# Attention and mixture of experts on one core: row stores released inside the score products, weight splits and half row sums on GpSimd

## The chip, the cores and the metric

The kernel runs on one core of a Trainium2 chip. The metric is the device time of one execution in microseconds (us). Before the change it is 597.46 us, the median of 3 runs (596.34 to 598.12). Engines are named as in the profile: PE is TensorE's matmuls, PEld its weight loads, DVE is VectorE, ACT ScalarE, POOL GpSimd, SP the engine that issues most loads.

## The reference

Two stages. Attention works on chunks of 64 tokens, 8 batches of 8 heads with 576 tokens of 64 values. Its output, 4608 rows of 512, goes to 8 experts, one for each row:

```python
scores = scale * np.matmul(q_c, k_c.transpose(0, 1, 2, 4, 3))
scores = scores - np.max(scores, axis=-1, keepdims=True)
attn = np.exp(scores)
attn = attn / (np.sum(attn, axis=-1, keepdims=True) + 1e-09)
out = np.matmul(attn, v_c)
...
expert_idx = np.argmax(logits, axis=1)
...
for e in range(E):
    mask = expert_idx == e
    xe = x[mask]
    h = np.maximum(xe @ w1[e], 0.0)
    ye = h @ w2[e]
    out[mask] = gate_w[mask, None] * ye
```

## The kernel before

**Stages.** The attention loop has 18 iterations, numbered `g` from 0 to 17. Each takes two tiles of 128 rows. A short tail follows in which the last tiles are routed while TensorE already multiplies for the first expert slot, and then the expert stage: slots of 256 rows, grouped by expert through an index table, with the weights loaded per slot. Rows are written to `xd` in DRAM by an indirect DMA that GpSimd issues (`store`, L435), so that they lie in the order of their experts, and are gathered again for the slots (L558).

**Order.** PE, DVE, ACT and POOL run the program in the order in which it is written. Only SP's queue of loads is put in order by the scheduler. Each engine works its queue strictly from the front, so an instruction that waits holds up all behind it.

**One iteration.** The loop is a pipeline. Iteration `g` computes the score products of its own tiles (`scores`, L240, into the tile `psS`, which lies in two PSUM banks), transposes the softmax of iteration `g-1` (L285, copied to `at` by ACT, L286), transposes the rows of iteration `g-2` (L317, copied to `xT`, L319), multiplies attention and v for `g-1` (L294), and computes the gate's logits for `g-2` (L329, copied to `lp`, L968). The product with `sel_g` (L959) at the start of an iteration, behind the score products on PE, reads the `lp` of the iteration before.

The softmax is spread over three engines. DVE takes the row maxima `mx` from `psS` (L253) and subtracts them into `ex` (L256); ACT computes Exp in place (L262). In the next iteration DVE sums the rows of `ex` (`soft_c`, L266) into `su`, ACT adds 1e-9 to the 16 sums (`soft_e`, L272), DVE takes the reciprocal `ri` (L277) and scales the products into a row buffer (L306). DVE then does a few small steps of the routing (L357 to L412, L493 to L525), up to five between the subtraction and `ri` and some more behind L306.

On ACT the order in an iteration is: two copies `at`, two copies `xT`, `soft_e`, Exp, the casts of weights (L86), `lp`, small routing steps, and then the first instruction of the next iteration's store.

**Stores.** From iteration 7 on, two row tiles that are routed are stored in each iteration. So that they don't leave early, ACT first copies one value of the new score tile into an unused last column of the first of the two rows (L433), which the DMA reads. It is called right behind `scores(g)`.

**First weights.** The weights of the first slot arrive in 16 pieces of 128x512 in two buffers `raw` (L981, one load in each of iterations 0 to 6, the others from iteration 12 on in the program's text). `split_half` turns each into a high part (ACT, L86) and a low part, which POOL subtracts at once (L88, same iteration). The tables `loads` and `splits` give the iterations: one piece in each of 1 to 8, one in 14, two in 15 and two in 16.

In iteration 15, right behind that iteration's stores, POOL also issues the first gather, `gather(0)` (L558, two DMAs), which reads rows of `xd` that the stores just ahead of it write, and whose target is a buffer that those stores read.

Of the kernel before, what the change touches and what calls it, by code (L numbers as in the profile page):

```python
# [8 lines left out]
F32 = mybir.dt.float32  # L9
# [4 lines left out]
ALU = mybir.AluOpType  # L14
AX = mybir.AxisListType
# [3 lines left out]
P = 128  # L19
# [6 lines left out]
NG = NTILE // G  # L26
# [12 lines left out]
XW = D + 16  # L39
# [8 lines left out]
def attn_moe_kernel(ctx: ExitStack, tc: tile.TileContext, q, k, v, wg, w, out):  # L48
    nc = tc.nc

    const = ctx.enter_context(tc.tile_pool(name="const", bufs=1))
# [16 lines left out]
    raw = [wpool.tile([P, 2048], F32, name=f"raw{c}") for c in range(2)]  # L68
# [11 lines left out]
    def split_half(j, eng):  # L80

        c, m = j // 2, j % 2
        hi, lo = w_hi[0][c][:, m * 512:(m + 1) * 512], w_lo[0][c][:, m * 512:(m + 1) * 512]
        o = (c % 2) * 1024 + m * 512
        src = raw[j // 4 % 2][:, o:o + 512]
        nc.scalar.copy(hi, src)  # L86
        yield
        eng.tensor_tensor(lo, src, hi.bitcast(F32), ALU.subtract)  # L88
# [133 lines left out]
    def quads(i, hp):  # L222
        for c in range(2):
            for m in range(2):
                o = hp * 128 + c * 64
                yield (slice(c * 64, (c + 1) * 64), m, slice((i * 4 + hp) * 64, (i * 4 + hp + 1) * 64),
                       slice(m * 64, (m + 1) * 64), slice(o, o + 64), (m * 64, c * 64))
# [7 lines left out]
    def scores(g):  # L235
        ps = pair
        for i in range(G):
            for hp in range(4):
                for po, m, fo, pi, fi, at_ in quads(i, hp):
                    nc.tensor.matmul(ps[po, m, fo], qt[g][pi, i, fi], kb[g % NK][pi, i, fi],  # L240
                                     start=True, stop=True, tile_position=at_)
        return ps

    NH = 2 * G * 4

    def heads(x):

        return x.rearrange("p m (h k) -> p (m h) k", k=64)

    def soft_a(ps):  # L250
        mx = sm.tile([P, NH, 1], F32, name="mx", bufs=2)
        ps3 = heads(ps)
        nc.vector.tensor_reduce(mx.rearrange("p h o -> p (h o)"), ps3, AX.X, ALU.max)  # L253

        ex = sp.tile([P, NH // 2, 2, 64], F32, name="ex", bufs=2)
        nc.vector.tensor_tensor(  # L256
            ex.rearrange("p h m k -> p m h k"), ps.rearrange("p m (h k) -> p m h k", k=64),
            mx.rearrange("p (m h) o -> p m h o", m=2).broadcast_to([P, 2, NH // 2, 64]), ALU.subtract)
        return ex
# [1 line left out]
    def soft_b(ex):  # L261
        nc.scalar.activation(ex, ex, AF.Exp, scale=0.125)  # L262

    def soft_c(ex):
        su = sm.tile([P, NH, 1], F32, name="su", bufs=2)
        nc.vector.tensor_reduce(su.rearrange("p (m h) o -> p m (h o)", m=2),  # L266
                                ex.rearrange("p h m k -> p m h k"), AX.X, ALU.add)
        return su

    def soft_e(su):  # L270
        suf = su.rearrange("p h o -> p (h o)")
        nc.scalar.activation(suf, suf, AF.Copy, bias=1e-9)  # L272
# [7 lines left out]
    def attn_t(ex, banks="UV"):  # L280
        at = sp.tile([P, G, 4, 128], F32, name="at", bufs=1)
        for i in range(G):
            pt = bank(banks, [P, 4, 128])
            for hp in range(4):
                nc.tensor.transpose(pt[:, hp, :], ex[:, i * 4 + hp, :, :].rearrange("p m k -> p (m k)"), ident)  # L285
            nc.scalar.copy(at[:, i, :, :], pt)  # L286
        return at
# [24 lines left out]
    def x_t(g, xt):  # L312
        xT = sp.tile([P, 4, G * P], F32, name="xT1", bufs=1)
        for i in range(G):
            pxt = bank("TQ", [P, 4, 128])
            for kc in range(4):
                nc.tensor.transpose(pxt[:, kc, :], xt[:, (g * G + i) % RB, kc * 128:(kc + 1) * 128],  # L317
                                    ident)
            nc.scalar.copy(xT[:, :, i * P:(i + 1) * P], pxt)  # L319
        return xT  # L320
# [103 lines left out]
            active.append([g, next(g), True])  # L424

    waiting = []

    def store(n, after=None):

        for k, (b, i, t, di) in enumerate(waiting[:n]):  # L430
            x = xb[t // RB % XB][:, t % RB, :]
            if k == 0 and after is not None:
                nc.scalar.copy(x[:, XW - 1:XW], after)  # L433
            stored.add(t)
            nc.gpsimd.indirect_dma_start(  # L435
                out=xds[t],
                out_offset=bass.IndirectOffsetOnAxis(ap=di[:, i, :], axis=0),
                in_=x, in_offset=None, bounds_check=NT - 1, oob_is_err=False)
        del waiting[:n]
# [4 lines left out]
    def advance(kind, side=False):  # L444


        for x in active:
            if x[1] == kind and x[2] == side and not (kind == "t" and r_live[0]):
                x[1] = next(x[0], "end")
                if x[1] == "end":  # L450
                    active.remove(x)
                return
# [493 lines left out]

    cpl = const.tile([P, E + 2 * NU], F32, name="cpl")

    st_e, st_l, st_x = {}, {}, {}
    pls = [None]  # L950

    def sel_(g):
# [18 lines left out]
    def pauses():  # L971
        for x in list(active):
            if x[1] is None:
                x[1] = next(x[0], "end")
                if x[1] == "end":
                    active.remove(x)
# [9 lines left out]
    def cast(g):  # L986

        for j in splits.get(g, ()):
            list(split_half(j, nc.gpsimd))
        for j in loads.get(g, ()):  # L990
            load_q(j)

# [2 lines left out]
    for g in range(NG):  # L995
        ga, gl = g - 1, g - 2
        pace[0] = 1000
        ps = scores(g)
        keep((12, 6, 0)[min(g, 2)])

        store(2 if g + 1 < NG else 4, ps[:, 0, 0:1])
        if gl >= 1:
            sel_(gl - 1)
            advance("c")
        if ga >= 0:
            at = attn_t(st_e[ga])
            su = soft_c(st_e.pop(ga))
        if gl >= 0:
            st_x[gl] = x_t(gl, xb[gl * G // RB % XB])
        if ga >= 0:  # L1010
            soft_e(su)
        st_e[g] = soft_a(ps)
        if g + 1 < NG:
            soft_b(st_e[g])
        else:

            c2.close()
            psum.append(ctx.enter_context(tc.tile_pool(name="psum", bufs=1, space=PSUM)))
        pauses()
        cast(g)  # L1020
        advance("t")
        if g + 1 < NG:
            small_op(5)
        if ga >= 0:
            px = attn_v(ga, at)
        logits(gl)
        if g + 1 == NG:
            soft_b(st_e[g])
        if ga >= 0:
            ri = soft_d(su)  # L1030
            x_out(ga, px, ri, xb[ga * G // RB % XB])
        small_op(2)
        advance("a")
        side_op(4)
        if g + 3 < NG:
            load_qk(g + 3)
        if 3 <= g + 2 < NG:
            load_v(g + 2)

    g = NG - 1  # L1040
# [4 lines left out]
    ex = st_e.pop(g)  # L1045
    at = attn_t(ex, "TQ")
    filler(1)
    su = soft_c(ex)
    soft_e(su)
    advance("a")  # L1050
# [240 lines left out]
```

## Time and profile before

One execution was profiled. Its own time is 601.14 us, its span, from the first to the last instruction, 599.2 us, at a mean granted TensorE clock of 0.976.

| What | Value |
|---|---|
| median of 3 runs | 597.46 us |
| profiled execution: time, span | 601.14 us, 599.2 us |
| HBM read, written | 121.60 MB, 19.82 MB |
| split by POOL (L88), 128x512 | 13 times, 1277 ns each |
| row stores (L435) | 36 DMAs, 0.97 to 1.15 us of POOL each |
| score products start (iteration 0, iteration 17) | 4.78 us, 124.97 us |

How to read the rows in the prediction: a group's row has line, engine, operation, output and inputs with shapes, count, then busy time in all and mean time of one in ns, then the idle time of the engine just before them and what ended it. A row of the timeline has its start, its length, engine, line, operation, and in brackets the idle time before it and what released it. "issue" means that the engine waited for nothing that the profile shows. Matmul records in a row of scores count 64 for the 32 products of an iteration, two for each.

### The profile page before, as it was taken

What the parts mean: (1) busy time and instruction counts of PE and PEld (TensorE: products, weight loads), DVE (VectorE), ACT (ScalarE), POOL (GpSimd) and SP (SyncE); (2) the same over time, 40 slices, a digit from 0 to 9 for tenths busy, and PEclk for the clock granted to TensorE, in tenths of its full rate; (3) what the DMA queues carried; (4) which work ended last, traced back from release to release, by engine and by line L of the source; (5) the groups of instructions that cost most, each with busy time, mean ns of one, the idle gap of its engine ahead of it and who ended that gap; (6) DMA issues with size and microseconds to landing.
All of it is one profiled execution on the core that took longest, in us unless ns stands there. A gap on an engine that the chain in (4) does not pass through costs nothing.

```text
span 599.2 us, 14785 instructions
## 1 busy us (share of the span) xinstructions
PE 563.4 (94%) x5603; PEld 497.4 (83%) x5603; DVE 445.9 (74%) x849; ACT 299.3 (50%) x562; POOL 261.2 (44%) x276
## 2 busy tenths in 40 slices
PE   7788788988999999999999999999998999999995
PEld 4676667776889889989899888998997899899894
DVE  7769687896668687786677678788655878777975
ACT  2656464675124555554455455555434555555552
POOL 3214332385645355434364445535424263464352
PEclk9989797999899999999999999999999999999998
DMA  8989897833467462357226622358633135623021
GB/s 296 383 306 333 285 373 231 294 117 142 160 205 250 144 225 81 108 175 230 59 68 235 205 58 71 103 190 319 217 93 99 45 112 191 205 76 101 20 57 37
DMA packets 59701, 103.31 MB, mean 172 GB/s; under 512 B 16240, under 2 KB 32624, under 8 KB 55984
## 3 DMA queue, kind: packets, MB, share of 16 engines
q0 software_dynamic: 20704, 60.74, 30.0%
q1 hardware_dynamic: 38864, 40.94, 21.2%
q8 instruction: 67, 1.10, 0.8%
q14 instruction: 66, 0.54, 0.3%
HBM read 121.60 MB, written 19.82 MB: 236 GB/s over the span
## 4 chain that ended last, share of the span: by engine, by line
PE 61%; DMA 10%; issue 2%; POOL 2%; POOLq 1%; DVE 1%; ACT 1%; ACTq 0%
PE psS L624 15%; DMA out_y<-y,oid 10%; PE psS L631 7%; PE psV L703 5%; PE psU L703 4%; PE psU L704 4%; PE psL L624 4%; PE psU L705 4%; PE psV L704 4%; PE psV L705 4%; PE psL L631 2%; POOLq L1229 1%; PE psK L717 1%; PE psK L719 1%; POOL out_y L731 1%
## 5 line engine op out<-in xcount | busy, mean ns | idle before, releaser
L78 DVE TENSOR_TENSOR wlo<-raw,whi 128x1024 fp32r<-128x1024 f32 x134 | 163.7, 1221 | 27.0 <-ACT whi L77 18.2
L77 ACT CAST whi<-raw 128x1024 fp32r<-128x1024 f32 x134 | 140.1, 1046 | 0.2 <-issue 0.2
L540 POOL DMA_INDIRECT raw<-in_w,widx x70 | 78.6, 1123 | 101.1 <-DVE wlo L78 37.2
L645 ACT ACTIVATE hh<-psS 128x256 fp32r<-128x256 f32 x110 | 42.3, 384 | 160.9 <-PE psS L624 105.3
L731 POOL DMA_INDIRECT out_y<-y,oid x40 | 50.5, 1262 | 112.3 <-ACT y L728 31.2
L624 PE MATMUL psS<-xhi,whi 128*128 128x256 f32 x344 | 98.0, 285 | 0.2 <-issue 0.2
L624 PE MATMUL psS<-xlo,whi 128*128 128x256 f32 x344 | 97.8, 284 | 0.3 <-DVE xlo L583 0.3
L624 PE MATMUL psS<-xhi,wlo 128*128 128x256 f32 x344 | 97.6, 284 | 0.0
L558 POOL DMA_INDIRECT xg<-xd,idx x58 | 71.4, 1231 | 28.9 <-issue 18.5
L650 DVE SCALAR_TENSOR_TENSOR hl<-psS,hh 128x256 fp32r<-128x256 f32 x110 | 46.4, 422 | 42.8 <-ACT hh L645 25.2
L624 PEld LDWEIGHTS psS<-xhi,whi 128*128 128x128 f32 x344 | 66.0, 192 | 4.0 <-issue 0.4
L624 PEld LDWEIGHTS psS<-xlo,whi 128*128 128x128 f32 x344 | 66.1, 192 | 3.3 <-DVE xlo L583 0.5
L624 PEld LDWEIGHTS psS<-xhi,wlo 128*128 128x128 f32 x344 | 66.0, 192 | 0.0
L703 PE MATMUL psU<-whi,hh 128*128 128x512 f32 x144 | 57.4, 398 | 1.6 <-ACT whi L77 1.6
L703 PE MATMUL psV<-whi,hh 128*128 128x512 f32 x144 | 57.9, 402 | 0.8 <-issue 0.6
L704 PE MATMUL psU<-wlo,hh 128*128 128x512 f32 x144 | 57.1, 397 | 0.0
L704 PE MATMUL psV<-wlo,hh 128*128 128x512 f32 x144 | 56.7, 394 | 0.0
L705 PE MATMUL psV<-whi,hl 128*128 128x512 f32 x144 | 56.4, 392 | 0.0
L705 PE MATMUL psU<-whi,hl 128*128 128x512 f32 x144 | 56.4, 392 | 0.0
L435 POOL DMA_INDIRECT xd<-xb,di x32 | 31.6, 986 | 39.3 <-issue 26.2
L88 POOL TENSOR_TENSOR wlo<-raw,whi 128x512 fp32r<-128x512 f32 x13 | 16.5, 1277 | 47.4 <-ACT whi L86 33.9
L240 PEld LDWEIGHTS psS<-kb,qt 64*64 64x64 f32 x1152 | 19.5, 135 | 18.1 <-issue 12.6
(252 smaller groups left out, 1209.5 us busy)
## 6 DMA issues: line engine op xcount, KB each, us to landing
kb<-in_k SPq DMA_DIRECT2D x36, 256.0 KB
qt<-in_q SPq DMA_DIRECT2D x36, 256.0 KB
vb<-in_v SPq DMA_DIRECT2D x36, 256.0 KB
xg<-xg SPq DMA_DIRECT2D x256, 32.0 KB
raw<-in_w SPq DMA_DIRECT2D x16, 256.0 KB
raw<-in_w,widx POOLq DMA_INDIRECT x70
xg<-xd,idx POOLq DMA_INDIRECT x58
out_y<-y,oid POOLq DMA_INDIRECT x40
```

What stands on the lines that cost most here:

```text
L77: nc.scalar.copy(hi, src)
L78: nc.vector.tensor_tensor(lo, src, hi.bitcast(F32), ALU.subtract)
L540: nc.gpsimd.indirect_dma_start(out=raw[c][:, :], out_offset=None, in_=w, in_offset=bass.IndirectOffsetOnAxis(ap=widx[:, u, c:c + 1], axis= ...
L558: nc.gpsimd.indirect_dma_start(out=t[:, :], out_offset=None, in_=xd[0:rows, :], in_offset=bass.IndirectOffsetOnAxis(ap=place(u, h), axis=0 ...
L624: nc.tensor.matmul(ph, a, b[:, kc, 0:BLK], start=kc + i == 0, stop=kc + i == 5)
L631: nc.tensor.matmul(ph, a[par][kc][:, f * 128:(f + 1) * 128], b[:, kc, 0:BLK + n], start=kc + i == 0, stop=kc + i == 5)
L645: nc.scalar.activation(hh, ph, AF.Relu)
L650: nc.vector.scalar_tensor_tensor(hl, ph, 0.0, hh.bitcast(F32), ALU.max, ALU.subtract)
L703: nc.tensor.matmul(py, hh, wh, start=f == 0, stop=False)
L704: nc.tensor.matmul(py, hh, wl, start=False, stop=False)
L705: nc.tensor.matmul(py, hl, wh, start=False, stop=f == 7)
L731: nc.gpsimd.indirect_dma_start(out=outs[m], out_offset=bass.IndirectOffsetOnAxis(ap=oid[u % 3][0:n, m:m + 1], axis=0), in_=y, in_offset=No ...
```

## The change

Five edits, all in the attention loop:

1. `store` is called inside `scores`, behind the first four of the 32 products, instead of behind all of them. In `store` POOL copies the marked column into a small tile `relay` before it issues the DMAs.
2. POOL adds the two halves of each row of `ex` (32 values each) into a quarter of a `raw` buffer that is free at that time (`halve`), behind the Exp of the same iteration.
3. DVE's `soft_c` sums these 32 values instead of 64.
4. `soft_c` and `soft_e` stand behind `soft_a` (maximum and subtraction) of the new scores instead of ahead.
5. POOL's subtraction for a weight piece is issued one iteration after ACT's cast. The copies of ACT stay where they were.

```diff
@@ scores
+                if i == 0 and hp == 0:
+                    store(2 if g + 1 < NG else 4, ps[:, 0, 0:1])
         return ps
...
+    def halve(g, ex):
+
+        c, j = (1, 3) if g < 6 or 12 < g < 15 else (0, 3 if g < 15 else 0)
+        h = raw[c][:, j * 512:(j + 1) * 512].rearrange("p (h m k) -> p h m k", m=2, k=32)
+        nc.gpsimd.tensor_tensor(h, ex[:, :, :, 0:32], ex[:, :, :, 32:64], ALU.add)
+        return h
+
-    def soft_c(ex):
+    def soft_c(h):
         su = sm.tile([P, NH, 1], F32, name="su", bufs=2)
         nc.vector.tensor_reduce(su.rearrange("p (m h) o -> p m (h o)", m=2),
-                                ex.rearrange("p h m k -> p m h k"), AX.X, ALU.add)
+                                h.rearrange("p h m k -> p m h k"), AX.X, ALU.add)
...
+    relay = const.tile([P, 1], F32, name="relay")
...
                 nc.scalar.copy(x[:, XW - 1:XW], after)
+                nc.gpsimd.tensor_copy(relay, x[:, XW - 1:XW])
...
         for j in splits.get(g, ()):
-            list(split_half(j, nc.gpsimd))
+            casts.append(split_half(j, nc.gpsimd))
+            next(casts[-1])
...
-        store(2 if g + 1 < NG else 4, ps[:, 0, 0:1])
...
         if ga >= 0:
-            at = attn_t(st_e[ga])
-            su = soft_c(st_e.pop(ga))
+            at = attn_t(st_e.pop(ga))
         if gl >= 0:
             st_x[gl] = x_t(gl, xb[gl * G // RB % XB])
+        st_e[g] = soft_a(ps)
         if ga >= 0:
+            su = soft_c(st_h.pop(ga))
             soft_e(su)
-        st_e[g] = soft_a(ps)
...
         pauses()
+        for x in casts:
+            next(x, None)
+        casts.clear()
         cast(g)
+        if g + 1 < NG:
+            st_h[g] = halve(g, st_e[g])
```

PE has the same rows in the same order; what differs is a wait. Here is PE's queue at the score products of iteration 7, the first with a store, with the semaphores that a row waits for. Before:

```order
L240 MATMUL psS<-kb_128,qt 64x64 [waits DMAHW7_49,DMAHW0_49,DVE_49]
L240 MATMUL psS<-kb_128,qt 64x64 x15
L240 MATMUL psS<-kb_128,qt 64x64 [waits DMAHW2_49,DMAHW1_49]
L240 MATMUL psS<-kb_128,qt 64x64 x15
L959 MATMUL psL<-sel_g,lp 128x8 [waits Activation_49]
L959 MATMUL psL<-sel_g,lp 128x8
L285 MATMUL psU<-ident,ex 128x128 [waits DVE_49]
```

And after, where L971 is the former L959 and L294 the former L285:

```order
L240 MATMUL psS<-kb_128,qt 64x64 [waits DMAHW7_49,DMAHW0_49,DVE_49]
L240 MATMUL psS<-kb_128,qt 64x64 x3
L240 MATMUL psS<-kb_128,qt 64x64 [waits Activation_49]
L240 MATMUL psS<-kb_128,qt 64x64 x11
L240 MATMUL psS<-kb_128,qt 64x64 [waits DMAHW2_49,DMAHW1_49]
L240 MATMUL psS<-kb_128,qt 64x64 x15
L971 MATMUL psL<-sel_g,lp 128x8 x2
L294 MATMUL psU<-ident,ex 128x128 [waits DVE_49]
```

The fifth product now waits for ACT, which reads the score tile for the store's copy, and the wait ahead of `sel_g` is gone. ACT's own rows and their order are the same in both.

DVE at the change from iteration 15 to 16, before (`add` and `g` are routing steps):

```order
L306 TENSOR_TENSOR xb_125<-psV,ri 128x2x256
L516 TENSOR_SCALAR add_239<-c_1833 128x1
L522 TENSOR_SCALAR add_239<-add_239 128x1
L525 TENSOR_SCALAR g_241<-pid_h,add_239 128x3
L266 TENSOR_REDUCE su<-ex 128x16
L253 TENSOR_REDUCE mx<-psS 128x16
L256 TENSOR_TENSOR ex<-psS,mx 128x2x8x64
L357 TENSOR_REDUCE lm<-lg 128x4
```

And after, with L255, L258 and L275 for the former L253, L256 and L266:

```order
L315 TENSOR_TENSOR xb_125<-psV,ri 128x2x256
L527 TENSOR_SCALAR add_240<-c_1853 128x1
L533 TENSOR_SCALAR add_240<-add_240 128x1
L536 TENSOR_SCALAR g_242<-pid_h,add_240 128x3
L255 TENSOR_REDUCE mx<-psS 128x16
L258 TENSOR_TENSOR ex<-psS,mx 128x2x8x64
L275 TENSOR_REDUCE su<-raw_66 128x16
L366 TENSOR_REDUCE lm<-lg 128x4
```

The sum has moved behind the subtraction and reads what POOL wrote into `raw`.

POOL from the stores of iteration 15 on, through the first gather, to the routing of iteration 16 (`ft` is a routing value that POOL copies into the rows). Before:

```order
L435 DMA xd<-xg_64,di 4608x528 x2
L558 DMA xg_64<-xd,idx_235 128x528 x2
L88 TENSOR_TENSOR wlo_4_80<-raw_66,whi_4_72 128x512
L88 TENSOR_TENSOR wlo_5_81<-raw_66,whi_5_73 128x512
L414 COPY xg_64<-ft 128x2x2
```

And after, with L444 to L446 for the store, L270 for `halve` and L569 for the gather:

```order
L444 COPY relay<-xg_64 128x1
L446 DMA xd<-xg_64,di 4608x528 x2
L569 DMA xg_64<-xd,idx_236 128x528 x2
L88 TENSOR_TENSOR wlo_4_80<-raw_66,whi_4_72 128x512
L270 TENSOR_TENSOR raw_66<-ex 128x512
L423 COPY xg_64<-ft 128x2x2
```

One split instead of two stands behind the gather, and behind it the addition for iteration 15, whose result DVE reads in iteration 16.

More of the change, by code (lines that the diff above doesn't have):

```diff
@@ L947, in attn_moe_kernel @@
     cpl = const.tile([P, E + 2 * NU], F32, name="cpl")
-    st_e, st_l, st_x = {}, {}, {}
+    st_e, st_h, st_l, st_x = {}, {}, {}, {}
+    casts = []
     pls = [None]
```

## Prediction

> **What bounds the kernel now.** I read the page first, then busy time stage by stage, then the chain that ended last inside the one stage that the change edits, then the rows at its stalls. From the page, the share of each engine and the 40 slices:
>
> ```profile
> PE 563.4 (94%) x5603; PEld 497.4 (83%) x5603; DVE 445.9 (74%) x849; ACT 299.3 (50%) x562; POOL 261.2 (44%) x276
> ...
> PE   7788788988999999999999999999998999999995
> ...
> PEclk9989797999899999999999999999999999999998
> DMA  8989897833467462357226622358633135623021
> ```
>
> A slice is 15 us. From slice 11 on TensorE is busy to 9 tenths or more; the expert stage, which the change doesn't touch, follows at its pace. What the attention loop (the first nine slices, 18 iterations, to about 132 us) ends later or earlier is therefore carried to the end one for one. The question is what sets the pace there. Busy time by stretch, one iteration of the loop each (length first, then PE, PEld, DVE, ACT, POOL busy with counts, granted clock, DMA share, GB/s):
>
> ```profile
> 63.28:70.97 7.69, 7.69 (x158) 6.81 (x157) 5.17 (x11) 4.78 (x11) 3.05 (x4) 0.64 0.86 278
> 70.97:77.17 6.20, 5.80 (x170) 5.06 (x165) 5.90 (x13) 3.86 (x10) 2.79 (x6) 1.00 0.73 239
> 77.17:83.73 6.56, 5.64 (x164) 4.75 (x157) 5.66 (x8) 3.75 (x8) 1.96 (x2) 1.00 1.01 380
> ...
> 93.18:101.47 8.29, 8.29 (x167) 7.57 (x166) 5.22 (x15) 4.09 (x10) 2.41 (x5) 0.62 0.59 200
> 101.47:107.59 6.12, 5.71 (x161) 4.71 (x156) 5.19 (x9) 3.75 (x8) 1.96 (x2) 1.00 0.91 304
> ...
> 113.64:120.71 7.07, 6.17 (x172) 5.21 (x166) 6.74 (x15) 4.73 (x13) 2.79 (x3) 1.00 0.76 273
> ```
>
> In iterations 9 and 13 (the rows from 70.97 and from 101.47) TensorE has 0.4 us of idle time in 6.2 and 6.12: its own program sets the spacing, with VectorE close behind. In the last iterations VectorE and then ScalarE take over, as the chain that ended last shows:
>
> ```profile
> 121.25 1.12 DVE su L266
> 122.37 1.14 DVE mx L253
> 123.53 1.24 DVE ex L256
> 124.79 1.06 ACT ex L262
> ...
> 126.26 0.61 ACT whi L86
> 126.88 0.28 ACT lp L968
> 127.20 0.61 PE psL L959 x4
> ```
>
> Row sum, maximum, subtraction, Exp, two weight casts, the copy lp, and only then TensorE's next product. The first 93 us have a third limit: TensorE stops in the middle of a run of products, where no semaphore is awaited (the releaser is "issue"), in stretches where DMA is full (1.01 and 380 GB/s in the row from 77.17).
>
> ```profile
> 62.88 0.47 PE L240 MATMUL psS<-kb,qt 64*64 64x64 f32 x2 [3.81 <-issue]
> ...
> 87.98 0.27 PE L294 MATMUL psU<-vb,at 64*64 64x64 f32 x1 [1.56 <-issue]
> ...
> 92.89 0.36 PE L240 MATMUL psS<-kb,qt 64*64 64x64 f32 x1 [2.21 <-issue]
> ```
>
> At 62.88 only the last 2 of 64 score records were missing, so it isn't a late q or k. After the two long ones the clock falls (0.64 in the row from 63.28, 0.62 in that from 93.18).
>
> **The change, part by part.** All times below are positions in the profiled execution; its span is 599.2 and its time 601.14, 3.7 above the median of 597.46, so I carry only the difference over to the median.
>
> *VectorE's row sum of half the width.*
>
> ```profile
> L266 DVE TENSOR_REDUCE su<-ex 128x16 f32<-128x1024 f32 x17 | 20.6, 1210 | 1.1 <-ACT ex L262 1.1
> L306 DVE TENSOR_TENSOR xb<-psU,ri 128x512 f32<-128x512 f32 x15 | 10.4, 692 | 8.7 <-PE psV L294 5.6 <-PE psU L294 2.5
> ```
>
> A sum over 512 elements isn't in the trace. Half of 1210 ns is 0.60; no gain at all is 1.21; VectorE's pass over 512 elements at L306 takes 0.69. I take 0.67, so 0.54 us less in each of 17 iterations: 9.2 us of VectorE's time. It reaches the end only where VectorE is the last to arrive, and the next part takes that away.
>
> *The store's copy inside the score products.* The order shows that from iteration 7 on the fifth product waits for ScalarE: the 1-column copy reads the score tile that the products still write. Before, only the maximum waited for the copy, and it was usually later anyway.
>
> ```profile
> 76.08 1.16 PE L240 MATMUL psS<-kb,qt 64*64 64x64 f32 x64
> ...
> 77.31 0.16 ACT L433 COPY xb<-psS 128x1 f32<-128x1 f32 x1 [0.56 <-PE psS L240]
> ...
> L240 PE MATMUL psS<-kb,qt x1152: 218/218/366, 4.8 to 125.9; 64*64 64x64 f32 x192
> ```
>
> TensorE must let the first products drain (0.22, one record), the copy begins 0.07 after the last product ends (76.08 + 1.16 = 77.24 to 77.31) and takes 0.16, and TensorE resumes about 0.05 later, as it does after lp in the chain (127.16 to 127.20). That is **0.50 us per iteration** in which TensorE stands still with everything queued behind: the other products, the transposes, attention times v. The bounds are 0 (nothing held) and the time until ScalarE's queue gets there, next part.
>
> *Row sum moved behind the subtraction, Exp behind it.* ScalarE's order is unchanged: the small su step (L272) still stands ahead of Exp. So Exp now waits for the halved sum (0.67), a hand-over (0.08) and the spacing from su to Exp (0.12): 0.87 later after the maximum than before. Behind Exp stand casts, lp and the copy that TensorE now awaits:
>
> ```profile
> 118.30 1.06 ACT L262 ACTIVATE ex<-ex 128x1024 f32<-128x1024 f32 x1 [1.32 <-DVE ex L256]
> 119.26 1.12 ACT L86 CAST whi<-raw 128x512 fp32r<-128x512 f32 x2
> 120.29 0.36 ACT L968 COPY lp<-psL 128x256 f32<-128x256 f32 x1
> ...
> 120.68 0.17 ACT L433 COPY xg<-psS 128x1 f32<-128x1 f32 x1
> ```
>
> This closes a loop from the end of one set of products to the end of the next: 0.05 to the maximum, 2.51 to Exp as before (122.28 to 124.79), 0.87 more, 2.38 from Exp to the store's copy with two casts (118.30 to 120.68), 0.21 for copy and hand-over, and the other 56 of 64 records, 1.02. That is 7.04 us with two casts (iterations 15 and 16), 6.52 with one (a cast is 0.52, half of 119.26 to 120.29), 6.01 with none.
>
> *GpSimd.* An addition of 128x512 is not there, but the split's subtraction of the same size is: 1277 ns. I take 1.27; the bounds are 0.6 and 2.5 (a strided read at half the rate). In most iterations POOL has room for it (1.96 to 3.05 us busy of 6 to 8, in the rows above) and the split, now an iteration late, is needed much later. The exception is iteration 15, where the addition queues behind a gather that waits for row stores to land:
>
> ```profile
> 116.05 0.98 POOL L435 DMA_INDIRECT xd<-xg,di  x1 [0.30 <-issue]
> 120.95 1.05 POOL L558 DMA_INDIRECT xg<-xd,idx  x1 [3.92 <-DVE add L516]
> 122.31 1.01 POOL L558 DMA_INDIRECT xg<-xd,idx  x1 [0.30 <-PE psV L285]
> 123.35 2.51 POOL L88 TENSOR_TENSOR wlo<-raw,whi 128x512 fp32r<-128x512 f32 x2
> ...
> L88 POOL TENSOR_TENSOR wlo<-raw,whi 128x512 fp32r<-128x512 f32 x13 | 16.5, 1277 | 47.4 <-ACT whi L86 33.9 <-DMA raw<-in_w 13.6
> ```
>
> Gathers until 123.35, one split until 124.6, the addition until 125.9. VectorE wants it in iteration 16. The relay copies are small (ScalarE's 1-column copy takes 0.16) and stand ahead of stores that nothing awaits but that gather: nothing.
>
> *Transfers.* Two of the 16 weight loads move from the crowded stretch to iterations 13 and 15, where DMA has room; SP waits there for the sum, with v loads behind it that are used two iterations later: nothing. In the two iterations with long stalls the stores leave earlier by about the stall (3.81 and 2.21 us), two times 128 x 528 words, 0.54 MB, among full queues: between 0 and 1.4 us more at 380 GB/s, against 0.7 less for a weight load gone. I take 0.
>
> **Sum.** Scores start at
>
> ```profile
> 100.37 1.16 PE L240 MATMUL psS<-kb,qt 64*64 64x64 f32 x64
> ...
> 112.55 1.16 PE L240 MATMUL psS<-kb,qt 64*64 64x64 f32 x64
> ...
> 124.97 1.16 PE L240 MATMUL psS<-kb,qt 64*64 64x64 f32 x64
> ```
>
> so they are 6.15 apart (24.60 over four). Scores of iteration 13 end 0.5 later; 14: another 0.5 (6.65 against the loop's 6.01); 15: another 0.5 (6.65, loop 6.52). They ended at 113.71 (112.55 + 1.16), now at 115.2. With two casts behind them the loop takes over: scores of 16 end at 115.2 + 7.04 = 122.25. VectorE then wants the addition at 122.25 + 2.44 = 124.7 and gets it at 125.9, 1.2 late. Scores of 17 end at 122.25 + 7.04 + 1.2 = 130.5, where TensorE's next step began at 127.20: **+3.3**. Iterations 7 to 12 add 0 to 2.0 (four holds; in 8 and 12 the stall hides it); TensorE's stalls there (1.56 and 2.21 in the rows above) are waits for something that comes at its own time and swallow most, so I take 0.2. Together +3.5: 604.6 against 601.14 profiled, **601.0** against the median 597.46.
>
> **Rivals.**
>
> *Slower by more, the clock.* Before scores 17 resume, TensorE stands idle for some 2.0 us (first products ready at 127.6, copy at 129.6). In this trace idle times of 3.81 and 2.21 us were followed by a stretch at 0.64 and 0.62, one of 1.56 (87.98) was not. The price is that of such a stretch, 7.69 instead of 6.20 or 8.29 instead of 6.12, so 1.5 to 2.2: 602.5 to 603.2. [...]
>
> *Slower by more, VectorE held up.*
>
> ```profile
> 70.08 1.27 POOL L88 TENSOR_TENSOR wlo<-raw,whi 128x512 fp32r<-128x512 f32 x1 [3.31 <-ACT whi L86]
> ...
> 70.64 0.78 DVE L374 TENSOR_TENSOR lo<-am,iota_m 128x48 bf16<-128x48 f32 x1
> ...
> 90.28 0.20 DVE L374 TENSOR_TENSOR lo<-am,iota_m 128x48 bf16<-128x48 f32 x1
> ```
>
> A step of 0.20 took 0.78 and ended at 71.42, just after POOL's subtraction (71.35). Seventeen more such spans can hit it, or its neighbours, in five iterations, at up to 1.07 each: +5.4 at most, if VectorE is last there; I expect it not to be, so 603 with little chance. [...]
>
> *No change.* The copy's hold is hidden by other waits and the addition comes in time. Against it: 0.4 us of idle time in iterations 9 and 13 leave little to hide behind. Even without any hold, the late addition alone would put Exp of 16 at 126.8 instead of 124.79. With POOL in time and no hold the last iterations give 1.12 - 0.87 = 0.25 back: 597.2.
>
> *Faster, the other side.* The long stall before 62.88 (3.81 us) hangs on what else the queues carry. If the load that left the stretch, or VectorE's shorter program, shifts it so that it stays under some 2 us, the stall shrinks by 2 to 3.8 and the slow-clock stretch behind it goes too (1.5): -3.5 to -5.3, with the +3.5 of the sum 595.7 to 597.5. Should the one before 92.89 go as well (2.21, and 2.2 for its slow stretch), some 592. For it: the price per stall is high. Against: they come where DMA is full, and the bytes hardly change.
>
> **How the numbers follow.** Forecast 0.40 (599.5 to 603.5), clock 0.17, VectorE held 0.05, no change 0.21, faster 0.17. A measurement here can tell about 0.3% from no change, 1.8 us: slower is 599.3 and above, faster 595.7 and below. From the forecast's lower edge and the rivals: slower 0.60, same 0.24, faster 0.16. The range is 594.5 to 606.0: below, one stall and its slow clock gone; above, the unswallowed holds (1.8) and the clock (1.5 to 3).
>
> **What would show it.** Right: from iteration 7 on each set of score products is cut after 8 records by about 0.5 us, waiting for the copy; starts from iteration 13 on are 6.6 to 7 apart; VectorE waits for POOL's addition in iteration 16; the last lp comes about 3 us later relative to iteration 12. Wrong: products that run through, a sum that isn't near 0.67, or stalls before the scores of iterations 8 and 12 that differ by more than 1 us from 3.81 and 2.21.

## The result and the profile after

| | before | changed |
|---|---|---|
| median | 596.9 us (593.77 to 598.12, 4 runs) | 604.88 us (598.88 to 607.7, 4 runs) |
| ratio, 95% interval | | 1.014 (1.0094 to 1.0186) |
| the same again, another set of runs (e5) | 595.52 us (23 runs) | 603.32 us (6 runs), 1.0126 (1.0091 to 1.016) |
| profiled span | 599.2 us | 605.7 us |

The change makes the kernel about 8 us slower. The ratios, here and below, leave out slow runs, those over 1.5% above the fastest of their kernel; the medians hold all runs. The page of the changed kernel, busy time first, then TensorE's slices and its granted clock:

```profile
PE 567.4 (94%) x5603; PEld 501.4 (83%) x5603; DVE 439.0 (72%) x849; ACT 299.3 (49%) x562; POOL 293.5 (48%) x308
...
PE   8888797878999999999999999999999999999995
...
PEclk9979797987999999999999999999999999999999
```

VectorE is 6.9 us less busy, GpSimd 32 us more. The halved sums and the additions as groups (line, engine, operation, shapes, count, busy and mean ns, idle before):

```profile
L270 POOL TENSOR_TENSOR raw<-ex 128x512 f32<-128x512 f32 x17 | 21.6, 1270 | 57.0 <-ACT ex L264 49.4 <-DVE ri L286 7.5
L275 DVE TENSOR_REDUCE su<-raw 128x16 f32<-128x512 f32 x17 | 11.5, 676 | 1.9 <-POOL raw L270 1.9
```

Both are priced as predicted (1.27 and 0.67 us). Now some of the score products from iteration 10 on, from the timeline of TensorE (start, length, the idle time before and its releaser):

```profile
78.82 1.04 PE L240 MATMUL psS<-kb,qt 64*64 64x64 f32 x56 [0.42 <-ACT xb L443]
...
109.47 1.04 PE L240 MATMUL psS<-kb,qt 64*64 64x64 f32 x56 [0.57 <-ACT xb L443]
...
123.31 0.92 PE L240 MATMUL psS<-kb,qt 64*64 64x64 f32 x47 [0.91 <-ACT xg L443]
...
132.32 1.38 PE L240 MATMUL psS<-kb,qt 64*64 64x64 f32 x56 [3.25 <-ACT xb L443]
```

All 11 sets from iteration 7 on are cut after 8 records and wait for ScalarE's copy: 0.41 to 0.58 us in seven of them, 1.18 and 1.02 in iterations 7 and 8, and in the last two rows above (iterations 16 and 17) 0.91 and 3.25. The same stretch on the other engines, iterations 16 and 17, in order of time:

```profile
124.90 1.22 DVE L255 TENSOR_REDUCE mx<-psS 128x16 f32<-128x1024 f32 x1 [1.42 <-PE psS L240]
126.16 1.22 DVE L258 TENSOR_TENSOR ex<-psS,mx 128x1024 f32<-128x1024 f32 x1
127.62 1.27 POOL L270 TENSOR_TENSOR raw<-ex 128x512 f32<-128x512 f32 x1
128.92 0.69 DVE L275 TENSOR_REDUCE su<-raw 128x16 f32<-128x512 f32 x1 [1.54 <-POOL raw L270]
129.64 0.21 ACT L281 ACTIVATE su<-su 128x16 f32<-128x16 f32 x1 [1.68 <-DVE su L275]
129.76 1.04 ACT L264 ACTIVATE ex<-ex 128x1024 f32<-128x1024 f32 x1
130.71 1.12 ACT L86 CAST whi<-raw 128x512 fp32r<-128x512 f32 x2
132.13 0.14 ACT L443 COPY xb<-psS 128x1 f32<-128x1 f32 x1
```

This is the forecast's loop, row for row: VectorE is done with the subtraction at 127.38 and waits 1.54 us for the addition that stands behind the gather, Exp waits for the sum, the casts stand behind Exp, the copy behind them, and TensorE behind the copy. What the forecast's sum did not have comes next, in the tail. Stretches of the changed kernel (length, then PE, PEld, DVE, ACT, POOL busy, granted clock, DMA share, GB/s):

```profile
130.00:132.30 2.30, 0.00 (x0) 0.00 (x0) 2.14 (x7) 2.27 (x6) 1.64 (x2) 1.00 0.14 57
132.30:135.00 2.70, 2.68 (x63) 2.56 (x64) 1.36 (x2) 0.00 (x0) 2.70 (x4) 0.60 0.41 152
135.00:138.00 3.00, 3.00 (x16) 2.94 (x15) 1.96 (x3) 1.76 (x3) 2.74 (x4) 0.50 0.02 6
138.00:141.00 3.00, 2.69 (x80) 2.05 (x78) 1.05 (x3) 0.95 (x3) 2.19 (x3) 0.72 0.48 186
```

After the stop of 3.25 us TensorE runs at a granted clock of 0.50 for 6.8 us, from 132.85 to 139.67. And then, timeline of VectorE, GpSimd and TensorE:

```profile
141.62 2.70 DVE L410 TENSOR_SCALAR gs<-gs 128x4 f32<-128x4 f32 x1
141.74 2.53 POOL L88 TENSOR_TENSOR wlo<-raw,whi 128x512 fp32r<-128x512 f32 x2
...
145.05 0.36 PE L635 MATMUL psS<-xhi,whi 128*128 128x256 f32 x1 [1.34 <-DVE oid L584]
```

A step on 4 values per partition takes 2.70 us, from just before two of GpSimd's subtractions to just behind them, and TensorE's first product of the expert stage waits behind VectorE. The same two rows before the change:

```profile
133.65 0.17 DVE L401 TENSOR_SCALAR gs<-gs 128x4 f32<-128x4 f32 x1
...
134.87 0.35 PE L624 MATMUL psS<-xhi,whi 128*128 128x256 f32 x1 [0.19 <-issue]
```

**Two stretches hold nearly the whole effect.** Call A the time from the first score product of iteration 13 to the first `sel_g` product behind those of iteration 17, and B the time from there to the first product of the expert stage. Where iteration 13 starts is no measure: 95.2 to 102.8 in the 14 profiles of this study, by the stalls that come before. All times in us:

| kernel | A | B | A + B | change of A + B | ratio of the times, interval |
|---|---|---|---|---|---|
| before | 26.83 | 7.67 | 34.50 | | |
| changed | 30.85 | 11.41 | 42.26 | +7.8 | 1.014 (1.0094 to 1.0186) |
| changed again (e5) | 30.26 | 11.18 | 41.44 | +6.9 | 1.0126 (1.0091 to 1.016) |
| e1 store behind | 29.19 | 15.66 | 44.85 | +10.4 | 1.0175 (1.0126 to 1.0223) |
| e6 no read | 27.91 | 8.96 | 36.87 | +2.4 | 1.0087 (1.006 to 1.0113) |
| e10 no read, Exp first | 27.30 | 9.92 | 37.22 | +2.7 | 1.0047 (1.0006 to 1.0089) |
| e11 no read, full sums | 26.54 | 7.49 | 34.03 | -0.5 | 0.997 (0.9937 to 1.0002) |
| e8 mended | 26.41 | 7.75 | 34.16 | -0.3 | 0.9972 (0.9942 to 1.0003) |
| e7 order alone | 26.91 | 9.66 | 36.57 | +2.1 | 1.0039 (1.0007 to 1.0072) |
| e2 store alone | 35.61 | 12.28 | 47.89 | +13.4 | 1.0288 (1.0244 to 1.0333) |
| e9 store alone again | 35.95 | 12.99 | 48.94 | +14.4 | 1.0228 (1.0151 to 1.0304) |
| e3 full sum 15 | 34.63 | 12.31 | 46.94 | +12.4 | 1.0285 (1.0234 to 1.0335) |
| e4 Exp first | 34.52 | 12.99 | 47.51 | +13.0 | 1.0256 (1.0209 to 1.0303) |
| e12 shift | 26.81 | 8.20 | 35.01 | +0.5 | 1.0018 (0.997 to 1.0066) |

One per cent is about 6 us, so the last two columns agree within 5 us in every row, though one is from a single profile and the other from 4 to 12 runs on three or more chips.

B falls into two parts, from that `sel_g` product to the next one and from there to the expert stage. Here they are before and in the changed kernel:

```profile
127.20:132.15 4.95, 4.46 (x100) 3.69 (x100) 4.88 (x8) 2.75 (x9) 4.48 (x6) 1.00 0.29 113
132.15:134.87 2.72, 2.53 (x20) 2.32 (x21) 2.39 (x8) 2.46 (x6) 2.11 (x3) 1.00 0.33 123
...
133.64:141.18 7.54, 7.05 (x104) 6.36 (x100) 4.37 (x6) 2.89 (x7) 6.46 (x8) 0.60 0.26 100
141.18:145.05 3.87, 2.53 (x21) 2.32 (x21) 3.83 (x7) 3.03 (x6) 3.21 (x4) 1.00 0.33 124
```

In the first part TensorE is busy 7.05 us instead of 4.46 and idle 0.49 in both; in the second it is busy 2.53 in both and idle 1.34 instead of 0.19.

### The profile page after: what moved, and what is told of

It is laid out like the page before. It is cut to its first block, busy times and chain, and to the rows that moved or that the text cites. A ratio compares the mean times of both kernels' runs of the same rounds, so it can differ in the third digit from the quotient of the medians.

```text
span 605.7 us, 14824 instructions
## 1 busy us (share of the span) xinstructions
PE 567.4 (94%) x5603; PEld 501.4 (83%) x5603; DVE 439.0 (72%) x849; ACT 299.3 (49%) x562; POOL 293.5 (48%) x308
## 4 chain that ended last, share of the span: by engine, by line
PE 45%; DMA 17%; issue 5%; POOL 4%; POOLq 3%; DVE 3%; ACT 0%; ACTq 0%
DMA out_y<-y,oid 10%; PE psS L635 10%; PE psS L642 6%; DMA raw<-in_w,widx 5%; PE psV L714 3%; PE psL L635 3%; PE psV L715 3%; PE psU L715 3%; PE psU L714 3%; PE psV L716 3%; PE psU L716 3%; POOLq L1246 3%; PE psL L642 2%; POOL raw L551 2%; POOL out_y L742 1%
## 5 line engine op out<-in xcount | busy, mean ns | idle before, releaser
L551 POOL DMA_INDIRECT raw<-in_w,widx x70 | 86.5, 1235 | 98.6 <-DVE wlo L78 46.6
L742 POOL DMA_INDIRECT out_y<-y,oid x40 | 52.5, 1312 | 105.8 <-ACT y L739 29.5
L569 POOL DMA_INDIRECT xg<-xd,idx x58 | 69.8, 1204 | 26.9 <-issue 20.5
L270 POOL TENSOR_TENSOR raw<-ex 128x512 f32<-128x512 f32 x17 | 21.6, 1270 | 57.0 <-ACT ex L264 49.4
L240 PEld LDWEIGHTS psS<-kb,qt 64*64 64x64 f32 x1152 | 21.5, 138 | 29.8 <-issue 14.4
L240 PE MATMUL psS<-kb,qt 64*64 64x64 f32 x1152 | 26.5, 229 | 20.6 <-issue 9.5
```

Source lines behind the costliest of these rows:

```text
L551: nc.gpsimd.indirect_dma_start(out=raw[c][:, :], out_offset=None, in_=w, in_offset=bass.IndirectOffsetOnAxis(ap=widx[:, u, c:c + 1], axis= ...
L569: nc.gpsimd.indirect_dma_start(out=t[:, :], out_offset=None, in_=xd[0:rows, :], in_offset=bass.IndirectOffsetOnAxis(ap=place(u, h), axis=0 ...
L742: nc.gpsimd.indirect_dma_start(out=outs[m], out_offset=bass.IndirectOffsetOnAxis(ap=oid[u % 3][0:n, m:m + 1], axis=0), in_=y, in_offset=No ...
```

## The experiments

**e1, the store behind the products again** (everything else as changed, no relay):

```diff
-                if i == 0 and hp == 0:
-                    store(2 if g + 1 < NG else 4, ps[:, 0, 0:1])
...
+        store(2 if g + 1 < NG else 4, ps[:, 0, 0:1])
```

> The changed kernel without edit 1: the store stands behind all 32 score products again and there is no relay copy; halved sums, their new place and the later splits stay. Measure: the stretch from the first score product of iteration 13 to the first sel_g product behind those of iteration 17 (26.83 us before, 30.85 changed). Theory (the held products and the late sum ahead of Exp add up): no set of products is cut any more, but Exp still waits for the sum and iteration 16 still waits about 1.5 us for the addition behind the gather, so the stretch is 28.2 to 29.2 and the whole about 600 to 602. Rival A (the hold is the whole cost): stretch within 0.4 of 26.83 and the whole time that of before. Rival B (the sum ahead of Exp is the whole cost, the hold hides beside it): stretch 30.4 or more, time as changed.

Measured 606.77 us, A 29.19: no set is cut, and A is what the theory said. Rivals A and B fall by their stretches. But the time is no better than the changed kernel's, where 600 to 602 was expected, since B is 15.66. VectorE and GpSimd in iteration 17 of e1:

```profile
125.33 4.28 DVE L381 TENSOR_TENSOR lo<-am,iota_m 128x32 bf16<-128x32 f32 x1
125.82 2.52 POOL L88 TENSOR_TENSOR wlo<-raw,whi 128x512 fp32r<-128x512 f32 x2
...
128.28 1.27 POOL L268 TENSOR_TENSOR raw<-ex 128x512 f32<-128x512 f32 x1
```

A step that takes 0.24 us elsewhere (132.06 in the changed kernel) takes 4.28: it lasts through two subtractions and the new addition, end to end. The maximum of iteration 17 begins at 129.75, 6.86 us after its products have ended. TensorE stops for 1.94 us behind that step, and the clock is at 0.50 from 131.00 to 141.24. The forecast had this mechanism as a rival of 0.05; here it is the largest single delay.

**e2 and e9, edit 1 alone** on the kernel before:

```diff
+                if i == 0 and hp == 0:
+                    store(2 if g + 1 < NG else 4, ps[:, 0, 0:1])
...
+                nc.gpsimd.tensor_copy(relay, x[:, XW - 1:XW])
...
-        store(2 if g + 1 < NG else 4, ps[:, 0, 0:1])
```

> The kernel before with edit 1 alone: the store inside the products, with the relay copy; sums full and in their old place. Theory: products are cut after 8 records from iteration 7 on, by 0.4 to 0.6 us where ScalarE is free and by 1 to 2 where it still does Exp and casts (iterations 7, 8, 16, 17); the stretch from iteration 13 to the sel_g products of 17 grows from 26.83 to 28.3 to 29.3, the whole by 1.5 to 3. Rival A (hold is the whole cost): stretch 30 or more. Rival B (hold hides beside other waits): stretch under 27.3, time that of before.

Measured 613.49 us, slower than the whole change, and A 35.61, far above the theory's 28.3 to 29.3. Rival A's figure (30 or more) fits it but its reason, the hold, doesn't: the sets are cut by 0.34 to 1.38 us, so the holds have about the size that the theory gave them. What is new is in rows like these of iteration 13 (TensorE, VectorE, ScalarE):

```profile
100.42 1.04 PE L240 MATMUL psS<-kb,qt 64*64 64x64 f32 x56 [0.42 <-ACT xb L436]
...
103.20 0.60 PE L319 MATMUL psQ<-ident,xb 128*128 128x128 f32 x4
103.46 1.22 DVE L255 TENSOR_REDUCE mx<-psS 128x16 f32<-128x1024 f32 x1 [1.57 <-PE psT L319]
104.22 0.58 ACT L288 COPY at<-psU 128x512 f32<-128x512 f32 x1 [3.86 <-issue]
```

The products end at 101.46 and VectorE was free at 101.89, but the maximum starts at 103.46; the transposes that ScalarE copies ended at 102.49, and the copy starts at 104.22. Before the change these lags are under 0.25 us. Here and in e3 and e4 such late signals come in about half of the held iterations, and in most of those ScalarE's copy starts 2.7 to 2.8 us after the last product, when TensorE has worked off all it had (its last transposes, in the row above, end 2.34 after the products). Where no stall or slow clock comes on top, these iterations take 7.2 to 8.4 us.

> The kernel of e2 once more (edit 1 alone on the kernel before), in another set of runs than e2, since e2, e3 and e4 showed late signals to VectorE and ScalarE that neither profile of the changed kernel has. If the late signals belong to the program, they are here again and the time is 611 to 615. If they belong to the circumstances of that set of runs (its chip), there are none, the stretch from iteration 13 to the sel_g products of 17 is 28 to 29.3, as first expected of e2, and the time 597 to 601.

Measured 612.34 us on another chip, with late signals in iterations 7 and 9 to 14 (in e2 in 9 to 14). So they are no accident of one set of runs. Whether they belong to the program isn't shown: e2 to e4 ran on chip 1 and e9 on chip 7, the changed kernel has no profile that is known to be from either (e5 ran on chip 0), and e3 has them in iterations whose instructions are the changed kernel's own. Their cause stays open.

**e3, VectorE sums iteration 15 in full**, in the changed kernel:

```diff
-            st_h[g] = halve(g, st_e[g])
+            st_h[g] = st_e[g] if g == 15 else halve(g, st_e[g])
```

> The changed kernel, but for the softmax of iteration 15 VectorE sums all 64 values itself (1.21 us), so that nothing waits for the addition that stands behind the gather. Theory: the wait of 1.54 us before the sum of iteration 16 goes and 0.54 comes back, so Exp of 16 starts 1.0 earlier, the hold in iteration 17 falls from 3.25 to about 2.2, and the stretch from 30.85 to 29.9; if the granted clock then stays up behind that hold, the whole gains another 1.7. Rival (ScalarE's queue, not the addition, sets the hold of 17): stretch unchanged within 0.3.

Measured 612.5 us, A 34.63: worse, which neither expected. The wait for the addition is gone (the sum starts at 127.50, right behind the subtraction), and the hold of iteration 17 is 0.40 us instead of 3.25. But late signals of up to 2.67 us appear from iteration 9 on, although every engine has the changed kernel's instructions in the same order up to the addition of iteration 15, the hold of iteration 16 grows to 2.62, and the clock falls there (0.58 in the 3 us from 124.09). The question was answered with e11 instead, where nothing is held.

**e4, Exp ahead of the step on su**, in the changed kernel:

```diff
-            soft_e(su)
         if g + 1 < NG:
             soft_b(st_e[g])
+            if ga >= 0:
+                soft_e(su)
         else:
+            soft_e(su)
```

> The changed kernel, but ScalarE does Exp ahead of its step on su, so Exp waits for neither the sum nor the addition. The store stays inside the products. Theory: Exp comes 0.05 behind the subtraction, 0.87 us earlier in each iteration and 2.4 earlier in iteration 16; the loop from products to products falls to 5.1 to 6.2 us, so that only the plain hold (0.4 to 0.6 an iteration, some 1 to 1.5 in 17) is left: stretch 27.8 to 28.8, the whole 2 to 4 us below the changed kernel. Rival (hold alone): stretch unchanged.

Measured 612.57 us, A 34.52, again with late signals (six iterations) and a hold of 2.58 in iteration 16. The same answer: what it asks was asked again without the hold, in e10.

**e5, the changed kernel again.**

> The changed kernel once more, beside the runs below and on one chip with them, to see what belongs to an execution and what to the program. The three runs with the store inside the products (e2, e3, e4) showed something that the first profile of the changed kernel does not: in about half of the held iterations VectorE's maximum began up to 2.66 us after the last product and ScalarE's copy of the transposes 1.7 us after them, with nothing else to wait for. If that belongs to the hold, it is to be seen here too, in some iterations from 7 on, and the time is 604 to 613. If it belongs to those programs, there is none of it here and the time is 602 to 607.

Measured 603.32 us and no late signals above 0.5 us in its profile: the second reading. Both parts of B's loss are there again: the clock is at 0.50 for 6.8 us behind a stop of 1.74, and the step on `gs` takes 2.65. It is the yardstick for e6.

**e6, no read of the score tile**: ScalarE's copy for the store reads `lp` of three iterations ago, at the same place in every queue.

```diff
-                    store(2 if g + 1 < NG else 4, ps[:, 0, 0:1])
+                    store(2 if g + 1 < NG else 4, st_l[g - 3][:, 0:1] if g > 2 else None)
```

> The changed kernel, but ScalarE's one-column copy for the store reads the logits lp of three iterations ago in SBUF instead of the score tile that the products are still writing. Queue orders, relay and place of the store stay; rows may leave a little earlier. Theory (the hold costs, by itself and by what follows it): no product waits for ScalarE, no late signals, stretch from iteration 13 to the sel_g products of 17 at most 29, time 2 to 5 us below the changed kernel of the same call. Rival (the late sum and the addition cost, the hold hides beside them): within 1.5 us of the changed kernel.

Measured 601.02 us, 2.3 below e5 on one chip, A 27.91 and B 8.96. No set is cut. By the profiles the hold costs 2.35 us in A and another 2.2 in B, where the granted clock now stays at 1.00. The times point the same way but don't settle it: the six runs of each overlap (599.25 to 602.81 against 599.39 to 605.64), so a difference within 1.5 us, the rival, isn't excluded by them. Some 5 us of loss by the ratio are left.

**e10, e6 with Exp first.**

> As e6 (ScalarE's copy for the store reads lp, so no product is held), and Exp goes ahead of the step on su; the additions of iterations 14 to 16 stay on GpSimd. Tells which half of e8's gain over e6 (6.4 us) is Exp's. Theory: Exp no longer waits for the addition behind the gather, so nearly all of it: 595 to 598. Rival (the additions in the last iterations cost through VectorE, which waits for them and is held up beside them): 599 to 601.

Measured 602.8 us against 600.23 of the kernel before on that chip, 1.0047 (the expected figures were for 595.52). The interval, 1.0006 to 1.0089, leaves theory and rival open; the rows don't. A falls by 0.6, B doesn't. ScalarE and VectorE in iteration 17, and TensorE behind them:

```profile
127.46 1.28 POOL L270 TENSOR_TENSOR raw<-ex 128x512 f32<-128x512 f32 x1
...
129.50 0.22 ACT L281 ACTIVATE su<-su 128x16 f32<-128x16 f32 x1 [3.46 <-DVE su L275]
129.62 0.35 ACT L980 COPY lp<-psL 128x256 f32<-128x256 f32 x1
130.02 0.61 PE L971 MATMUL psL<-sel_g,lp 128*128 128x8 f32 x4 [2.80 <-ACT lp L980]
...
133.25 3.19 DVE L584 SCALAR_TENSOR_TENSOR oid<-msk,xg 128x1 int32<-128x1 f32 x1
133.90 2.52 POOL L88 TENSOR_TENSOR wlo<-raw,whi 128x512 fp32r<-128x512 f32 x2
```

The addition for iteration 16 stands behind two splits, the sum waits for it, ScalarE's step on su for the sum, `lp` behind it on ScalarE, and TensorE 2.80 us for `lp`. Just behind B a step of 0.15 us takes 3.19 beside GpSimd's subtractions. That is the rival of this run, row by row.

**e11, e6 with full sums for iterations 14 to 16.**

```diff
-            st_h[g] = halve(g, st_e[g])
+            st_h[g] = st_e[g] if g > 13 else halve(g, st_e[g])
```

> As e6, and VectorE sums all 64 values for iterations 14 to 16; Exp still behind the step on su. The other half of e8. Theory: Exp waits for the sum (1.21 in place of 0.67) but for no addition, and GpSimd doesn't hold VectorE in the tail: 598 to 600. Rival: 595 to 597, if the additions were the whole loss of e6.

Measured 597.41 us against 600.23, 0.997: by the ratio nothing of the loss is left, the rival. The product for `lp` that came 7.24 us after the first `sel_g` product of stretch B in e10 comes 4.82 after it here. The late additions, three of 17, were the rest of the loss: e6 differs from this run in nothing else, and the intervals of the two (from 1.006 on, and up to 1.0002) don't meet.

**e8, all three mended** (e6, Exp first, full sums for 14 to 16).

> The changed kernel with three things mended: ScalarE's copy for the store reads lp instead of the score tile (as e6), Exp goes ahead of the step on su, and for iterations 14 to 16 VectorE sums all 64 values itself, so that nothing waits for GpSimd in the last iterations. Theory: nothing of the loss is left, time within 3 us of the kernel before, either side. Rival A (additions of GpSimd hold up VectorE elsewhere, or early stores cost transfers): 3 us or more above the kernel before.

Measured 594.6 us against 595.52, 0.9972: as the theory said. It and e11 beat the changed kernel; whether they beat the kernel before, their intervals, which end at 1.0003 and 1.0002, just don't say.

**e7, the new order alone**, on the kernel before: full sums behind the subtraction, Exp ahead of the step on su, no additions.

> The kernel before with one thing of the change: VectorE sums after the subtraction instead of ahead of the maximum, full width, and ScalarE does Exp ahead of its step on su. No additions on GpSimd, stores as before. Theory (VectorE's sum was on the path of the last iterations): the maximum starts 1.1 us earlier wherever VectorE came last (iterations 14 to 17), stretch 26.83 to 24.5 to 26, whole 1 to 2.5 us below the kernel before. Rival (reciprocal and scaling come late instead, since the sum now stands nearer to them): no difference that can be measured.

Measured 599.39 us, 1.0039. A is 26.91, as before. VectorE's sum was the first piece of the chain that ended last, 1.12 us long, and taking it off that place gains nothing: the rival's side, with 2 us lost in B. Just ahead of B TensorE stopped for 1.26 us (1.07 in the kernel before), and in it the clock was at 0.50 from 131.14 to 134.55. Why the clock fell there wasn't tried.

**e12, 16 more instructions for TensorE** in iteration 0:

```diff
-        keep((12, 6, 0)[min(g, 2)])
+        keep((20, 6, 0)[min(g, 2)])
```

> The kernel before with 8 more of the idle warm-up products (L232) in iteration 0, that is 16 more instructions in TensorE's queue (a weight load and a product each) ahead of everything, in a place where TensorE waits for loads. In all traces so far the long stalls in the score products of iterations 4, 8 and 12 stand before the last 3, 2 and 1 of the 64 records. Theory (the stall is where a block of TensorE's instructions begins, and has nothing to do with data): they move 8 records forward, to the last 11, 10 and 9. Rival (they wait for something that the products read): before the last 3, 2 and 1 as ever. Time within 3 us of the kernel before.

Its stalls in iterations 4, 8 and 12, from TensorE's timeline:

```profile
35.55 0.44 PE L240 MATMUL psS<-kb,qt 64*64 64x64 f32 x11 [2.84 <-issue]
...
65.40 0.69 PE L240 MATMUL psS<-kb,qt 64*64 64x64 f32 x10 [3.97 <-issue]
...
95.42 0.38 PE L240 MATMUL psS<-kb,qt 64*64 64x64 f32 x9 [2.57 <-issue]
```

Before the last 11, 10 and 9 records instead of the last 3, 2 and 1: the stall sits at a place in TensorE's stream of instructions, moves with it, and waits for no data. The time is that of the kernel before, 1.0018. What comes ahead of its end is in the traces too. The page of the profile lists a DMA queue that carries instructions (here that of the kernel before; packets, MB, share of 16 engines):

```profile
q8 instruction: 67, 1.10, 0.8%
```

Its packets have 16384 bytes each. In the 14 profiles TensorE stops 90 times for 0.7 us or more with no releaser between 10 and 130 us, and every one of these stops ends 1.05 to 1.64 us after such a packet has landed; before the row at 62.88, for one, it moved from 60.61 to 61.58. In the profiles of the kernel before and of the changed kernel these are 9 and 6 stops, which end 1.27 to 1.64 and 1.25 to 1.55 us after a landing. By these times the author takes them for waits for TensorE's next instructions; no row names what releases them.

## Why the prediction was right, and where it was too small

The sign was right and 604.88 lies in the range, but the forecast was +3.5 us and +8 came. By its own steps:

- **Row sum of half the width, addition: right.** 0.676 and 1.270 us against 0.67 and 1.27. The forecast's upper bound of 2.5 for the addition, a read at half the rate, was an estimate that no run shows. That VectorE's saving is taken away is right too; e7 and e11 add that it had nothing to give in the last iterations, since A stays at 26.5 to 26.9 with VectorE's sum behind the subtraction.
- **The hold of 0.50 us: right in size**, 0.41 to 0.58 in seven of eleven sets, and without it (e6) A is 2.35 us shorter than in e5. Whether the holds of iterations 7 to 12 are swallowed, as forecast, can't be read: iteration 13 starts at 102.79 and 95.51 in the two profiles of the changed kernel and at 95.21 to 101.75 in those without holds, and the stalls account for more than that.
- **Exp later by 0.87: 0.72.** Maximum to Exp is 3.23 us (110.98 to 114.21), 2.51 before.
- **The late addition of iteration 15: right**, 1.54 us of waiting against 1.2.
- **From iteration 13's start to the end of the last score products: 30.13 forecast** (130.5 - 100.37), 30.91 measured (102.79 to 133.70). Singly the spacings were off more: 5.77, 6.91, 6.59 and 6.67 instead of 6.6 to 7.
- **"What the attention loop ends later or earlier is therefore carried to the end one for one": this step failed.** The tail was taken as unchanged, and B grew by 3.74 us (3.51 in e5). By rows of the changed kernel: from one `sel_g` product to the next 7.54 us (133.64 to 141.18) where 4.95 stood before (127.20 to 132.15), so 2.59 for the slow clock, all of it TensorE's busy time; and 3.87 instead of 2.72 from there to the first product of the expert stage, so 1.15 for VectorE's step beside GpSimd, all of it TensorE's idle time. Nor is a late start handed on in full: from the first product of the expert stage to the end it is 464.4 us before and 460.6 in the changed kernel, and over the profiles 464.4 in the mean of the six that get there before 136 us and 462.0 in that of the eight others.

The first of these two is the rival on the clock, which had the chance of 0.17 and a price of 1.5 to 2.2. The forecast put TensorE's last idle time at 2.0 us, because it let TensorE reach the products of iteration 17 a microsecond later than it did; it came to 3.25. The copy that ended it was where the forecast had it, 7.3 us after the products of iteration 16. Behind that stop the clock fell (0.50 from 132.85), as in e5 behind a stop of 1.74 (124.11, clock 0.50 behind it). In the 3.41 us before the fall (the length of the shortest slow stretch in the profiles) TensorE was busy for 0.53 here and for 1.67 in e5, so it did not stand still throughout. The second is the rival on VectorE held up by GpSimd. It was priced within the loop, with little chance since VectorE would seldom be last there; its place is the tail, where GpSimd's splits, gathers, stores and additions come late and VectorE's routing steps and `oid` stand ahead of the first expert product.

A third thing was missed: "The exception is iteration 15." Iteration 16 is one too. Its addition stands behind two splits, and when the hold is taken away (e6, e10) it is what is late next, 2.80 us in e10.

The faster rival hung on a stall that shrinks. That of iteration 8 did, from 3.81 to 2.46 us, and that of iteration 12 grew from 2.21 to 3.58, both by more than the 1 us that the forecast had set as a sign against itself. But over all 14 profiles they range from 0.82 to 4.04 where there is one at all, and from 0.89 to 3.58 (in the two of the changed kernel 2.46 and none, 3.58 and 1.22), so such differences belong to the execution, and no such gain can be laid to the change.

That the time still lies in the range is in part luck. The range kept room above the forecast for unswallowed holds (1.8) and the clock (1.5 to 3); the clock took 2.59 of it, and the 1.15 of VectorE's step in the tail, for which none was kept, happened to fit beside that.

What is open: why edit 1 alone, e3 and e4 have late signals. In the profiles of the changed kernel there are none above 0.5 us, in e11 there is one, in an iteration with a stall and no hold, the rows name no cause, and chip and program were not varied one at a time. Open too is how much of the time the hold costs by itself, since e6's runs overlap with e5's.

## What to carry to other kernels

A marker that reads a tile while its producer is still writing it stopped the producer for 0.41 to 3.25 us a time in the changed kernel; read something that is already finished (e6) and the release costs no wait. Work moved to an engine "with room" has to be looked at in the iterations where that engine's queue is full: three of 17 additions cost most of what was left here, and they need not be moved at all (e11). And a stop of TensorE has to be priced with the slow clock behind it, which can cost as much as the stop (2.59 us behind one of 3.25, 2.25 behind that of 1.74 in e5).

## What the runs showed of the hardware

- **The clock after a stop.** In the 14 profiles TensorE stops 85 times for 1.3 us or more between 16 and 185 us. Taking the granted clock of the 3 us that begin 0.3 after the stop, it is under 0.9 after all 11 stops of 3 us or more, after 18 of 24 of 2 to 3 us, and after 22 of 50 of 1.3 to 2 us. So length alone does not decide below 3 us. The 61 slow stretches in that time, at a granted clock of 0.50, last 3.41, 6.83 or 10.24 us and begin, in each profile, on one grid of 3.41 us. Of the steps of this grid at a clock of 1.00, all 33 in which TensorE was busy for under 45% were followed by a clock of 0.50, 28 of 100 with 45 to 70%, and none of 462 with more (8 of 8, 1 of 8 and none of 64 in the profiles of the kernel before and of the changed kernel).
- **Stalls with no releaser** lie at fixed places of TensorE's instruction stream: before the last 3, 2 and 1 records of the products of iterations 4, 8 and 12 in every profile where they appear, and 8 records earlier with 16 more instructions ahead (e12). Their lengths vary from 0.8 to 4.0 us from one execution to the next. A packet of the instruction queue has 16384 bytes, and each of these stalls ends 1.05 to 1.64 us after one has landed (e12).
- **A VectorE step on a few values beside GpSimd's back-to-back steps** lasted from just before the first of them to just behind the last in three rows above: 2.70 (changed kernel), 3.19 (e10) and 4.28 us (e1), for steps that take 0.15 to 0.24 elsewhere. In e5 the step on `gs` took 2.65. That step has one input (`gs`, L410), and the one in e1 lasts from two subtractions into the addition. The maximum, which reads the score tile, ran beside two splits at its usual 1.22 before the change (129.51). Why the ones are held and the other isn't, the rows don't show.
